# Late values as quarter tiles joined to the next scores, loads ordered by their readers, and the first chunks' tiles kept in weight buffers

## The chip, the cores and the metric

The kernel runs on one core of a Trainium2 chip. The metric is the device time of the whole program in microseconds (us); a run of the kernel before takes 830.32 us (median of three).

## What is computed

Sliding-window attention with a linear bias over 4 batches, 8 heads, 576 positions and head size 64, then two MLPs over the 2304 tokens, all in fp32:

```python
scores = where(0 <= rel < 128, q @ k.T / sqrt(D) - slope_h * rel, -1e9)   # per batch and head
x = softmax(scores) @ v                       # heads side by side: 2304 x 512
h = x @ w_in                                  # 512 -> 2048
x = (max(h, 0) + alpha * min(h, 0)) @ w_out   # 2048 -> 512
h = max(max(x @ w1, x @ w2), x @ w3)          # 512 -> 768
out = h @ w_out2                              # 768 -> 512
```

## The kernel before

The tokens are cut into 9 chunks of 256, joined into five groups of one or two chunks. Attention works on pairs: one chunk and two neighbouring heads, so 36 pairs. For each pair TensorE does three pieces of work. The **scores** (L398) are 8 matmuls of 64 rows by 64 columns, each on one quarter of the array, with 192 moving columns. Then VectorE adds the bias and takes the row minimum (L412), ScalarE exponentiates (L418) and guards the sum (L423), VectorE inverts it (L426), and GpSimd scales the probabilities (L430). The **transposes** (L439) turn the probabilities over by 6 matmuls on the full array; ScalarE copies them to `pt` (L447). The **values** are 8 matmuls with all 128 rows and half of the columns (L459), then 8 on quarters (L466). ScalarE and VectorE split the result into a high and a low part in `x_a` (L479, L481), which the first MLP reads.

Every fp32 weight is likewise split into two parts (ScalarE L344, L346, L362; VectorE L348 to L354; GpSimd L357, L364), and a product of the MLPs is three matmuls (L515 to L517 for the hidden layer, L543 for its output). Jobs run over the hidden blocks f; an item of a job is one f for one or two chunks, that is 256 or 512 moving columns. The attention of chunk 0 stands ahead of the first item, chunk 1 lies within the first job, chunks 2 and 3 within the jobs up to the long one on group 1, and chunks 4 to 8 (`MERGED`) within the later jobs of the first MLP.

All buffers are rings or slots with a planner (`Plan`) that lists every operation with an engine, a cost and a due time, runs a list schedule in both directions for eight rounds, keeps the order with the earliest modelled end, and issues each engine's instructions in that order. Each engine then takes its instructions strictly in order. A buffer's first writer waits for the users of the buffer's last tenant, and, in a ring, also for the first writer of the tile made just before it. The rings that matter here: `qkv` holds the raw queries and keys of two pairs, `v` three, `pt` one, `sb` two PSUM banks. `attend` decides the order in which a pair's pieces are listed: the scores of the new pair, then the transposes and the values of the pair before it. The split weights have 32 buffers of their own, `w`. While the core waits at the start, `keep_busy` (L296) puts 24 matmuls of no use into TensorE's order. A new weight's load waits for the conversion of the fourth weight before it (`AHEAD`).

Of the kernel before, what the change touches and what calls it, by code (L numbers as in the profile page):

```python
# [8 lines left out]
F32 = mybir.dt.float32  # L9
# [61 lines left out]


class Op:
    def __init__(self, eng, cost, due, fn, deps, at, port):
        self.eng, self.cost, self.due, self.fn, self.deps, self.at = eng, cost, due, fn, deps, at
        self.port = port or eng == "pool"


class Plan:

# [8 lines left out]
        self.ops, self.free = [], free  # L89

    def add(self, eng, cost, due, fn, r=(), w=(), after=(), port=False):
        deps = set(after)
        assert not any(b.over for b in (*r, *w))
        for b in r:
            deps.update(b.writers)
        for b in w:
            if not b.writers:
                if b.last:
                    b.last.over = True
                    b.gate.update(b.last.writers, b.last.readers)  # L100
                if b.before and b.before not in w:
                    b.gate.add(b.before.writers[0])
            deps.update(b.gate)
            if b in r:
                deps.update(b.readers)
        op = Op(eng, cost, due, fn, deps, len(self.ops), port)
# [11 lines left out]

    def run(self, due, back=False):

        before, after = {op: list(op.deps) for op in self.ops}, {op: [] for op in self.ops}
        for op in self.ops:
            for d in op.deps:
                after[d].append(op)
        if back:
            before, after = after, before
# [2 lines left out]
        ready, start, end, dma, port = {e: [] for e in free}, {}, {}, 0.0, 0.0  # L129

        def release(op):
            t = max((end[d] + (self.lag(op, d) if back else self.lag(d, op)) for d in before[op]), default=0.0)
            ready[op.eng].append((t, op))

        for op in self.ops:
# [66 lines left out]

APART = (1,)

AHEAD = 4
LATER = 2

# [1 line left out]

KEEP = 3  # L210
ROUNDS = 8
WAIT = 0.08


# [10 lines left out]
def attention_then_two_mlps(ctx: ExitStack, tc: tile.TileContext, qkv, v, w_in, w_out, alpha, w123, w_out2, out):  # L225
# [15 lines left out]
    def either(name, *tiles):  # L241

        pool = ctx.enter_context(tc.tile_pool(name=name, bufs=1))
        return lambda form: pool.tile(*tiles[form], tag=name, name=f"{name}{'abc'[form]}")


    w_s = Slots([either(f"w{i}_", ([P, 2, 512], F32R), ([P, 1024], I32)) for i in range(2 * NF)])
# [4 lines left out]
    o_r = ring("o", 2, ([P, 512], F32))  # L252
    qkv_r = ring("qkv", 2, ([P, 10 * D], F32))
    v_r = ring("v", 3, ([P, 3, 2, D], F32))
    p_r = ring("p", 4, ([P, 2 * R], F32))
    z_r = ring("z", 2, ([P, 16], F32))
    pt_r = ring("pt", 1, ([P, 2, 2 * R], F32))
# [112 lines left out]
    def pair(k, j, hp, due):  # L370


        c = GROUPS[k][j]
        raw, vv, pt, z = qkv_r.new(), v_r.new(), pt_r.new(), z_r.new()
        qs, heads = slice(N + P, 2 * N + P), range(2)
        for a in heads:
            rows = slice(a * D, (a + 1) * D)
            load = add("sp", 0.6, due - 16, lambda a=a, rows=rows: nc.sync.dma_start(
                out=raw()[rows], in_=qkv[2 * hp + a, c, rows, :10 * D]), w=[raw])
# [9 lines left out]
        ps = [p_r.new() for _ in heads]  # L389


        def scores():
# [9 lines left out]
        scored = yield dict(cost=0.8, due=due - 12, fn=scores, r=[raw], w=s)  # L402
        if c == 0:
            idle_b.writers.append(scored)
            keep_busy(2 * KEEP, due - 2, [scored])


        exps = []
        for a in heads:
            for n in range(2):  # L410
                i, p, part = 2 * a + n, ps[a], slice(n * R, (n + 1) * R)
                least = add("dve", 0.28, due - 11 + a, lambda a=a, n=n, i=i, p=p, part=part: nc.vector.tensor_tensor_reduce(  # L412
                    out=p()[:, part], in0=s[a]()[:, part], in1=rel_of(4 * c + n),
                    op0=ALU.add, op1=ALU.min, scale=slope_of(2 * hp + a), scalar=3.0e38, accum_out=z()[:, i:i + 1]),
                    r=[s[a]], w=[p, z])
                if c == 0:
                    idle_b.readers.append(least)
                exps.append(add("act", 0.45, due - 10 + a, lambda i=i, p=p, part=part: nc.scalar.activation(  # L418
                    out=p()[:, part], in_=p()[:, part], func=AF.Exp, scale=-1.0, bias=z()[:, i:i + 1],
                    accum_out=z()[:, 4 + i:5 + i]), r=[p], w=[p, z], after=[least]))  # L420
        for a in heads:
            at_a, two = due - 8 + a, slice(2 * a, 2 * a + 2)
# [3 lines left out]
            share = add("dve", 0.08, at_a, lambda a=a: nc.vector.reciprocal(  # L426
                out=z()[:, 12 + 2 * a:14 + 2 * a], in_=z()[:, 8 + 2 * a:10 + 2 * a]), w=[z], after=[guard])
            for n in range(2):
                i, p, part = 2 * a + n, ps[a], slice(n * R, (n + 1) * R)
                z.readers.append(add("pool", 0.36, at_a + 0.2, lambda i=i, p=p, part=part: nc.gpsimd.tensor_scalar(  # L430
                    out=p()[:, part], in0=p()[:, part], scalar1=z()[:, 12 + i:13 + i], scalar2=1.0,
                    op0=ALU.mult, op1=ALU.mult), r=[p], w=[p], after=[share]))
        yield
        psts = [s_b.new() for _ in heads]
# [5 lines left out]

        if c not in MERGED:
            for a in heads:
                add("pe", 0.36, due - 6.5 + a, lambda a=a: transposes(a), r=[ps[a]], w=[psts[a]])
        else:
            add("pe", 0.7, due - 6, lambda: [transposes(a) for a in heads], r=ps, w=psts)
        for a in heads:
            add("act", 0.38, due - 5.5 + a, lambda a=a: nc.scalar.copy(pt()[:, a, :], psts[a]()[:, :2 * R]),  # L447
                r=[psts[a]], w=[pt])

        psv, at_q = (psts, 2 * R) if c not in APART else ([h_b.new() for _ in range(2)], 0)  # L450


        def values():

            for u in range(2):
                for n in range(2):
                    for a in heads:

                        nc.tensor.matmul(psv[n]()[a * D:(a + 1) * D, at_q + u * D:at_q + (u + 1) * D],  # L459
                                         vv()[:, u + n, a, :], pt()[:, a, n * 2 * P + u * D:n * 2 * P + (u + 1) * D],  # L460
                                         start=(u == 0), stop=False, skip_group_check=True)
            for u in range(2):
                for n in range(2):
                    for a in heads:
                        rows = slice(n * D, (n + 1) * D)
                        nc.tensor.matmul(psv[n]()[a * D:(a + 1) * D, at_q + u * D:at_q + (u + 1) * D],  # L466
                                         vv()[rows, u + 1 - n, a, :], pt()[rows, a, P + u * D:P + (u + 1) * D],
                                         start=False, stop=True, skip_group_check=True)

        yield dict(cost=0.95, due=due - 3.5, fn=values, r=[pt, vv, *(psv if at_q else [])], w=psv)  # L470
# [173 lines left out]
    def put(x):  # L644
        return add("pe", x["cost"], x["due"], x["fn"], r=x["r"], w=x["w"])

    def attend(i):

        for args in sorted(before.get(i, ()), key=lambda args: args is not None):
            new = args and pair(*args)  # L650
            if new:
                scores = next(new)
                new.send(put(scores))
            for one in going:
                put(next(one))
                next(one, None)
            going[:] = [new] if new else []

# [69 lines left out]
```

## Time and profile before

| what | value |
|---|---|
| median of 3 runs (lowest to highest) | 830.32 us (830.13 to 832.75) |
| time of the profiled execution | 833.15 us |
| its span, first to last instruction | 831.4 us |
| TensorE busy in it | 812.2 us |
| ScalarE, VectorE, GpSimd busy | 317.0, 445.6, 202.0 us |
| mean granted TensorE clock | 0.990 of full |

Two engines' busy times can't be added: they work side by side. TensorE is busy for nearly the whole span, so the table asks two questions of every part of the program: is TensorE waiting there, and if not, how long do its own instructions take? In the rows of a timeline, the first number is the start, the second the time from the first start to the last end, and xN counts records; an fp32 matmul of the program leaves two records. Records on one engine overlap, so the pace is read from starts, not from durations.

### The profile page before, as it was taken

The page shows a single profiled execution, that of the slowest core. Times are in us where ns is not written, and L with a number is a line of the kernel's source. Part 1 is how long each engine was busy: PE and PEld are TensorE (multiplying, and loading weights), DVE is VectorE, ACT ScalarE, POOL GpSimd, SP SyncE. Part 2 cuts the span into 40 slices and gives each one's busy share as a digit, 9 for nine tenths or more (in the row PEclk, how much of TensorE's full clock was granted, in tenths as well). Part 3 has the DMA queues.
Part 4 walks back from the last instruction along what each step waited for, and adds up shares of the span by engine and source line. Part 5 has one row for each costly group of instructions (what it writes and reads, how often), then busy time and mean ns, then how long its engine had stood idle before and what let it go on. Part 6 is the DMA issues. An engine that isn't in the chain of part 4 may idle for free.

```text
span 831.4 us, 14008 instructions
## 1 busy us (share of the span) xinstructions
PE 812.2 (98%) x5388; PEld 668.6 (80%) x5388; DVE 445.6 (54%) x1031; ACT 317.0 (38%) x858; POOL 202.0 (24%) x276
## 2 busy tenths in 40 slices
PE   7789999999999999999999999999999999999998
PEld 3678778888778999877787888888888888888897
DVE  4768989963544554544445699994232132222132
ACT  6989874410443443334333565442121121011111
POOL 5767674430121222122100234551000000000000
PEclk9789999999999999999999999999999999999999
DMA  8968530000211321111113774020020020010010
GB/s 241 307 229 264 179 99 14 1 1 0 92 43 52 103 71 53 54 40 43 36 36 122 248 215 140 1 89 13 1 103 1 0 89 13 0 64 13 1 52 26
DMA packets 28724, 65.42 MB, mean 79 GB/s; under 512 B 3824, under 2 KB 9456, under 8 KB 28656
## 3 DMA queue, kind: packets, MB, share of 16 engines
q1 hardware_dynamic: 28656, 64.51, 24.7%
q8 instruction: 43, 0.70, 0.4%
q14 instruction: 25, 0.20, 0.1%
HBM read 54.01 MB, written 10.49 MB: 78 GB/s over the span
## 4 chain that ended last, share of the span: by engine, by line
PE 92%; ACT 3%; DVE 3%; issue 1%; POOL 1%; DMA 0%; SPq 0%; POOLq 0%; DVEq 0%; ACTq 0%
PE xb L543 24%; PE xb L616 9%; PE hb L515 8%; PE hb L516 8%; PE hb L517 8%; PE hb L589 4%; PE sb L589 4%; PE hb L591 4%; PE sb L591 4%; PE sb L590 4%; PE hb L590 4%; PE sb L398 3%; PE sb L439 2%; PE sb L459 2%; PE sb L466 1%; ACT p L418 1%
## 5 line engine op out<-in xcount | busy, mean ns | idle before, releaser
L543 PE MATMUL xb<-g,w_a 128*128 128x512 f32 (+1 forms) x1008 | 221.4, 366 | 1.1 <-ACT g L494 1.1
L543 PEld LDWEIGHTS xb<-g,w_a 128*128 128x128 f32 x1008 | 168.5, 189 | 34.6 <-issue 5.6
L494 ACT CAST g<-hb 128x512 fp32r<-128x512 f32 (+1 forms) x99 | 52.3, 529 | 204.7 <-DVE hb L524 113.1
L515 PE MATMUL hb<-x_a,w_a 128*128 128x512 f32 (+1 forms) x336 | 124.7, 371 | 0.4 <-DVE g L495 0.3
L430 POOL TENSOR_SCALAR p<-p,z 128x192 f32<-128x192 f32 x144 | 66.0, 473 | 232.0 <-DVE z L426 219.0
L516 PE MATMUL hb<-x_a,w_a 128*128 128x512 f32 (+1 forms) x336 | 121.9, 363 | 0.0
L517 PE MATMUL hb<-x_a,w_a 128*128 128x512 f32 (+1 forms) x336 | 121.7, 362 | 0.0
L357 POOL TENSOR_TENSOR wt<-wt,w_b 128x512 int32<-128x512 int32 x56 | 79.5, 1422 | 116.1 <-DVE wt L354 101.1
L521 DVE TENSOR_SCALAR t<-hb,alpha_sb 128x512 f32<-128x512 f32 (+1 forms) x84 | 56.4, 671 | 80.1 <-PE hb L517 80.0
L495 DVE TENSOR_TENSOR g<-hb,g 128x512 fp32r<-128x512 f32 (+1 forms) x99 | 60.9, 616 | 36.7 <-ACT g L494 36.4
L418 ACT ACTIVATE p<-p,z 128x192 f32<-128x192 f32 x144 | 64.2, 447 | 38.6 <-DVE z L412 38.5
L616 PE MATMUL xb<-w_a,g 128*128 128x512 f32 x324 | 78.7, 390 | 0.0
L515 PEld LDWEIGHTS hb<-x_a,w_a 128*128 128x128 f32 x336 | 64.4, 192 | 14.2 <-issue 3.0
L517 PEld LDWEIGHTS hb<-x_a,w_a 128*128 128x128 f32 x336 | 64.5, 192 | 9.6
L516 PEld LDWEIGHTS hb<-x_a,w_a 128*128 128x128 f32 x336 | 64.6, 192 | 8.9
L616 PEld LDWEIGHTS xb<-w_a,g 128*128 128x128 f32 x324 | 60.5, 188 | 12.2
L590 PE MATMUL hb<-x_a,w_a 128*128 128x512 f32 (+1 forms) x180 | 66.3, 368 | 0.0
L591 PE MATMUL hb<-x_a,w_a 128*128 128x512 f32 (+1 forms) x180 | 66.3, 368 | 0.0
L590 PE MATMUL sb<-x_a,w_a 128*128 128x512 f32 (+1 forms) x180 | 66.3, 368 | 0.0
L591 PE MATMUL sb<-x_a,w_a 128*128 128x512 f32 (+1 forms) x180 | 66.3, 368 | 0.0
L589 PE MATMUL sb<-x_a,w_a 128*128 128x512 f32 (+1 forms) x180 | 66.2, 368 | 0.0
L589 PE MATMUL hb<-x_a,w_a 128*128 128x512 f32 (+1 forms) x180 | 66.2, 368 | 0.0
(71 smaller groups left out, 1074.2 us busy)
## 6 DMA issues: line engine op xcount, KB each, us to landing
qkv<-in_qkv SPq DMA_DIRECT2D x72, 160.0 KB, 3.0
w_b<-in_w_out SPq DMA_DIRECT2D x22, 512.0 KB, 5.9
w_b<-in_w SPq DMA_DIRECT2D x18, 512.0 KB, 4.2
w_b<-in_w_in SPq DMA_DIRECT2D x16, 512.0 KB, 6.2
v<-in_v SPq DMA_DIRECT2D x36, 192.0 KB, 2.4
x2d<-o SPq DMA_DIRECT2D x20, 256.0 KB, 2.6
out<-o SPq DMA_DIRECT2D x18, 256.0 KB, 2.1
o<-x2d SPq DMA_DIRECT2D x16, 256.0 KB, 2.9
```

Of the source, the lines that this page charges most:

```text
L357: add("pool", 1.27, due - 5, lambda: nc.gpsimd.tensor_tensor(out=wt().bitcast(I32), in0=wt().bitcast(I32), in1=words(0), op=ALU.add), r=[r ...
L418: exps.append(add("act", 0.45, due - 10 + a, lambda i=i, p=p, part=part: nc.scalar.activation(out=p()[:, part], in_=p()[:, part], func=AF. ...
L430: z.readers.append(add("pool", 0.36, at_a + 0.2, lambda i=i, p=p, part=part: nc.gpsimd.tensor_scalar(out=p()[:, part], in0=p()[:, part], s ...
L495: lo = add("dve", 0.07 + n / 960, due + 0.3, lambda: nc.vector.tensor_tensor(out=g()[:, 1, :n], in0=ps()[:, :n], in1=g()[:, 0, :n].bitcast ...
L515: nc.tensor.matmul(to, wi()[:, 0, ws], x[:, 0, cols], start=(kk == 0), stop=False)
L516: nc.tensor.matmul(to, wi()[:, 1, ws], x[:, 0, cols], start=False, stop=False)
L517: nc.tensor.matmul(to, wi()[:, 0, ws], x[:, 1, cols], start=False, stop=(kk == KD - 1))
L543: nc.tensor.matmul(to, wo()[:, a, ms], g()[:, b, :n], start=(opens and not a and not b), stop=(closes and ends), skip_group_check=apart)
L589: nc.tensor.matmul(to, w()[:, 0, ws], xk[:, 0, :n], start=(kk == 0), stop=False)
L590: nc.tensor.matmul(to, w()[:, 1, ws], xk[:, 0, :n], start=False, stop=False)
L591: nc.tensor.matmul(to, w()[:, 0, ws], xk[:, 1, :n], start=False, stop=(kk == KD - 1))
L616: nc.tensor.matmul(ps, g()[:, a, ts], w()[:, c], start=(opens and not a and not c), stop=(closes and ends))
```

## The change

There are five parts.

1. In the chunks of `MERGED` the values become 24 matmuls on quarters. The 128 keys that were contracted at once are cut into two halves of 64, so each quarter's rows go with one 64-query half. For that the probabilities are written in another order of columns (`part_of_p`), and a second tile `ve` brings the values of the middle part in the other halves of the partitions (two more loads a pair).
2. In those chunks `attend` takes the old pair's transposes first, and then lists the old pair's values and the new pair's scores as one TensorE operation into the same two PSUM banks. Where no pair follows, the values stand alone; where none came before, the scores do.
3. The raw queries and keys and the transposed probabilities of chunks 0 to 3 (`EARLY`) live in the eight last weight buffers, four for each, and not in the rings `qkv` and `pt`.
4. The neighbour in a ring no longer has to end first: it only has to start first (`behind`).
5. A load's due time comes from its earliest reader, 3 us ahead (`DMA_LEAD`). Some modelled costs change, and the order in which a job's last pair is closed.

```diff
@@ Plan.add, Plan.run, Plan.issue
-                if b.before and b.before not in w:
-                    b.gate.add(b.before.writers[0])
+                    behind.add(b.before.writers[0])
...
+                t = max((end[d] + self.lag(d, op) if d in op.deps else start[d] for d in before[op]), default=0.0)
...
+            users = {}
+            for op in self.ops:
+                for d in op.deps:
+                    if d.eng == "sp":
+                        users[d] = min(users.get(d, due[op]), due[op])
+            due.update((d, t - DMA_LEAD) for d, t in users.items())
@@ pair
-        raw, vv, pt, z = qkv_r.new(), v_r.new(), pt_r.new(), z_r.new()
+        vv, z = v_r.new(), z_r.new()
+        if c < EARLY:
+            raw, pt = (w_s.new(2 * NF - 8 + 4 * i + (c * KD + hp) % 4, 2 + i) for i in range(2))
+            ps = [p_r.new() for _ in range(2)]
+        else:
+            raw, pt, ps = qkv_r.new(), pt_r.new(), [p_r.new() for _ in range(2)]
...
+        ve = ve_r.new() if c in MERGED else None
+        if ve:
+            for n in range(2):
+                add("sp", 0.3, due - 9, lambda n=n: nc.sync.dma_start(
+                    out=ve()[n * D:(n + 1) * D], in_=v[hp, c, (1 - n) * D:(2 - n) * D, n * P:(n + 2) * P].rearrange(
+                        "p (k a d) -> p k a d", k=2, a=2)), w=[ve])
...
+        def part_of_p(p, n):
+            if not ve:
+                return p()[:, n * R:(n + 1) * R]
+            return p().rearrange("p (j n r) -> p n j r", n=2, j=3)[:, n]
...
+            def values(psv):
+
+                for u in range(2):
+                    for m in range(3):
+                        for n in range(2):
+                            for a in heads:
+                                rows, of = slice(n * D, (n + 1) * D), ve()[:, u] if m == 1 else vv()[:, u + m // 2]
+
+                                nc.tensor.matmul(psv[n]()[a * D:(a + 1) * D, 2 * R + u * D:2 * R + (u + 1) * D],
+                                                 of[rows, a, :], pt()[rows, a, m * P + u * D:m * P + (u + 1) * D],
+                                                 start=(u == m == 0), stop=(m == 2), skip_group_check=True)
@@ attend
-        for args in sorted(before.get(i, ()), key=lambda args: args is not None):
+        for args in before.get(i, ()):
             new = args and pair(*args)
-            if new:
-                scores = next(new)
-                new.send(put(scores))
+            late = new and going and GROUPS[args[0]][args[1]] in MERGED
+            if new and not late:
+                new.send(put(next(new)))
             for one in going:
-                put(next(one))
+                x = next(one)
+                scores = next(new) if late else None
+                if "w" not in x:
+                    banks, values = scores["w"] if late else [s_b.new() for _ in range(2)], x["fn"]
+                    x.update(fn=lambda: values(banks), w=banks)
+                if late:
+                    first = x["fn"]
+                    new.send(put(dict(cost=1.6, due=x["due"], fn=lambda: (first(), scores["fn"]()),
+                                      r=x["r"] + scores["r"], w=x["w"])))
+                else:
+                    put(x)
                 next(one, None)
```

How the order moves is seen at three places. The first is TensorE's queue in the job on group 2 (chunk 4's successor, one chunk of 256 columns an item). `sb` are the two PSUM banks, `pt` the transposed probabilities, `v` and `ve` the values, `hb` the next hidden block. Before, a pair's values stand by themselves:

```order
L459 MATMUL sb_3692<-pt_3714,v_3351 64x64 x2
L459 MATMUL sb_3696<-pt_3714,v_3351 64x64 x2
L459 MATMUL sb_3692<-pt_3714,v_3351 64x64 x2
L459 MATMUL sb_3696<-pt_3714,v_3351 64x64 x2
L466 MATMUL sb_3692<-pt_3714,v_3351 64x64 x2
L466 MATMUL sb_3696<-pt_3714,v_3351 64x64 x2
L466 MATMUL sb_3692<-pt_3714,v_3351 64x64 x2
L466 MATMUL sb_3696<-pt_3714,v_3351 64x64 x2
L515 MATMUL hb_3742<-x_a,w_a 128x256
```

After, the last six rows of a pair's values (L496) run straight into the next pair's scores (L426) in the same banks:

```order
L496 MATMUL sb_3903<-pt_3900,v_3586 64x64 x2
L496 MATMUL sb_3906<-pt_3900,v_3586 64x64 x2
L496 MATMUL sb_3903<-pt_3900,ve_3707 64x64 x2
L496 MATMUL sb_3906<-pt_3900,ve_3707 64x64 x2
L496 MATMUL sb_3903<-pt_3900,v_3586 64x64 x2
L496 MATMUL sb_3906<-pt_3900,v_3586 64x64 x2
L426 MATMUL sb_3903<-qkv_3685 64x192
L426 MATMUL sb_3906<-qkv_3685 64x192
```

The pass through the MLP's matmuls that stood between values and scores is gone, in 17 of the 20 pairs of `MERGED`; three values and three scores still stand alone.

The second place is ScalarE's queue in the same job. `p` are probabilities, `z` their sums, `g` a hidden block's high part. Before, a pair's exponentials (`p_3654`, `p_3661`) are followed by the copies of the pair before it, whose transposes (of `p_3532`) are in `sb_3692` and `sb_3696`:

```order
L418 ACTIVATE p_3654,z_3655<-p_3654,z_3655 128x192 x2
L418 ACTIVATE p_3661,z_3655<-p_3661,z_3655 128x192 x2
L423 ACTIVATE z_3655<-z_3655 128x2 x2
L447 COPY pt_3714<-sb_3692 128x384
L447 COPY pt_3714<-sb_3696 128x384
L494 CAST g_3719<-hb_3672 128x256
L479 CAST x_a<-sb_3692 128x2x64
L479 CAST x_a<-sb_3696 128x2x64
```

After, they are followed by the copies of the same pair: TensorE transposes `p_3813` into `sb_3877` and `p_3819` into `sb_3881`.

```order
L455 ACTIVATE p_3813,z_3814<-p_3813,z_3814 128x3x64 x2
L455 ACTIVATE p_3819,z_3814<-p_3819,z_3814 128x3x64
L460 ACTIVATE z_3814<-z_3814 128x2
L455 ACTIVATE p_3819,z_3814<-p_3819,z_3814 128x3x64
L460 ACTIVATE z_3814<-z_3814 128x2
L548 CAST g_3875<-hb_3830 128x256
L484 COPY pt_3900<-sb_3877 128x384
L484 COPY pt_3900<-sb_3881 128x384
L548 CAST g_3940<-hb_3887 128x256
```

So a pair's own softmax now lies between its scores and the next TensorE piece of attention, with 36 matmuls of 256 columns of the MLP between them in this job (32 the first time), where before a whole pair lay between. The first guard also moves ahead of the fourth exponential.

The third place is the start of SP's queue of loads. `qkv` or `w_c` are raw queries and keys (two loads a pair), `v` values, `w_b` a raw weight. Before:

```order
L378 DMA qkv_266<-in_qkv 64x640 x2
L382 DMA v_269<-in_v 128x384
L291 DMA alpha_sb<-in_alpha 128x16
L378 DMA qkv_273<-in_qkv 64x640 x2
L342 DMA w_b<-in_w_in 128x1024
L382 DMA v_297<-in_v 128x384
L378 DMA qkv_314<-in_qkv 64x640 x2
L342 DMA w_b<-in_w_out 128x1024
```

After:

```order
L400 DMA w_c<-in_qkv 64x640 x6
L404 DMA v_278<-in_v 128x384
L400 DMA w_c<-in_qkv 64x640 x2
L404 DMA v_297<-in_v 128x384
L404 DMA v_306<-in_v 128x384
L359 DMA w_b<-in_w_in 128x1024
L359 DMA w_b<-in_w_out 128x1024
L400 DMA w_c<-in_qkv 64x640 x2
```

All of chunk 0 now goes ahead of the first weight. Some rows further on, two pairs of chunk 4 (`qkv` and `ve`, loaded into rings that nothing else uses by then) stand before the fifth weight. The eight last weights now wait for the pairs whose tiles hold their buffers; the last load of a weight stands between the stores of the half-finished sum `x2d` at the end of the third job.

## Rows read from the trace of the kernel before

**Rows 1.** The page: span, and busy time of the engines.

```profile
span 831.4 us, 14008 instructions
PE 812.2 (98%) x5388; PEld 668.6 (80%) x5388; DVE 445.6 (54%) x1031; ACT 317.0 (38%) x858; POOL 202.0 (24%) x276
```

**Rows 2.** Busy time by stretch: length, five engines, TensorE's clock, DMA share, GB/s.

```profile
10.00:60.00 50.00, 42.21 (x503) 31.82 (x503) 35.98 (x132) 44.27 (x144) 34.74 (x50) 0.83 0.91 283
...
200.00:440.00 240.00, 240.00 (x2064) 197.36 (x2063) 115.17 (x369) 90.43 (x327) 40.91 (x98) 1.00 0.19 55
```

**Rows 3.** The same columns: both stretches at half clock, and the crowded stretch of loads.

```profile
26.40:36.60 10.20, 9.10 (x70) 7.36 (x71) 6.65 (x25) 8.28 (x26) 9.31 (x14) 0.50 1.04 331
53.70:60.50 6.80, 6.25 (x45) 4.63 (x45) 2.67 (x13) 4.23 (x17) 3.87 (x5) 0.50 0.51 178
...
5.00:55.00 50.00, 42.02 (x493) 29.87 (x497) 35.17 (x131) 44.09 (x145) 33.87 (x53) 0.88 0.96 297
```

**Rows 4.** TensorE's timeline around one pair's scores, and around its values.

```profile
218.12 0.39 PE L517 MATMUL hb<-x_a,w_a 128*128 128x512 f32 x1
218.44 0.88 PE L398 MATMUL sb<-qkv 64*64 64x192 f32 x16
219.25 0.50 PE L515 MATMUL hb<-x_a,w_a 128*128 128x512 f32 x1
219.58 0.40 PE L516 MATMUL hb<-x_a,w_a 128*128 128x512 f32 x1
219.82 0.39 PE L517 MATMUL hb<-x_a,w_a 128*128 128x512 f32 x1
...
224.71 0.69 PE L459 MATMUL sb<-pt,v 128*64 128x64 f32 x16
225.32 0.46 PE L466 MATMUL sb<-pt,v 64*64 64x64 f32 x16
225.71 0.96 PE L543 MATMUL xb<-g,w_a 128*128 128x512 f32 x3
```

**Rows 5.** Records of the attention's lines between 200 and 440 us (ns).

```profile
L398 PE MATMUL sb<-qkv x320: 322/323/374, 208.3 to 422.8; 64*64 64x192 f32 x160
...
L459 PE MATMUL sb<-pt,v x320: 221/222/271, 224.7 to 437.3; 128*64 128x64 f32 x160
...
L466 PE MATMUL sb<-pt,v x320: 217/218/268, 225.3 to 437.6; 64*64 64x64 f32 x160
```

**Rows 6.** Timelines of one softmax with 256 columns an item, and of another.

```profile
292.92 0.88 PE L398 MATMUL sb<-qkv 64*64 64x192 f32 x16
293.73 1.70 PE L543 MATMUL xb<-g,w_a 128*128 128x256 f32 x12
295.27 0.28 PE L515 MATMUL hb<-x_a,w_a 128*128 128x256 f32 x1
295.69 0.44 ACT L418 ACTIVATE p<-p,z 128x192 f32<-128x192 f32 x1
296.13 0.33 ACT L423 ACTIVATE z<-z 128x2 f32<-128x2 f32 x2
296.59 0.28 PE L517 MATMUL hb<-x_a,w_a 128*128 128x256 f32 x1
296.69 1.63 POOL L430 TENSOR_SCALAR p<-p,z 128x192 f32<-128x192 f32 x4 [5.10 <-DVE z L426]
...
286.10 0.74 PE L543 MATMUL xb<-g,w_a 128*128 128x256 f32 x4
...
289.51 1.62 POOL L430 TENSOR_SCALAR p<-p,z 128x192 f32<-128x192 f32 x4 [8.99 <-DVE z L426]
```

**Rows 7.** Timelines early on: ScalarE's fourth hidden block; SP's first weight and first store.

```profile
60.02 0.37 ACT L494 CAST g<-hb 128x256 fp32r<-128x256 f32 x1 [1.23 <-DVE hb L524]
...
4.24 0.58 SPq L342 DMA_DIRECT2D w_b<-in_w_in  x1
...
118.61 1.31 SPq L555 DMA_DIRECT2D x2d<-o  x2
```

More of the change, by code (lines that the diff above doesn't have):

```diff
@@ L91, in add @@
     def add(self, eng, cost, due, fn, r=(), w=(), after=(), port=False):
-        deps = set(after)
+        deps, behind = set(after), set()
         assert not any(b.over for b in (*r, *w))
@@ L105, in add @@
                 deps.update(b.readers)
-        op = Op(eng, cost, due, fn, deps, len(self.ops), port)
+        op = Op(eng, cost, due, fn, deps, behind, len(self.ops), port)
         for b in r:
@@ L119, in run @@
     def run(self, due, back=False):
-        before, after = {op: list(op.deps) for op in self.ops}, {op: [] for op in self.ops}
+        before, after = {op: [*op.deps, *op.behind] for op in self.ops}, {op: [] for op in self.ops}
         for op in self.ops:
-            for d in op.deps:
+            for d in (*op.deps, *op.behind):
                 after[d].append(op)
@@ L131, in release @@
         def release(op):
-            t = max((end[d] + (self.lag(op, d) if back else self.lag(d, op)) for d in before[op]), default=0.0)
+            if back:
+                t = max((end[u] + self.lag(op, u) if op in u.deps else end[u] - op.cost for u in before[op]), default=0.0)
+            else:
+                t = max((end[d] + self.lag(d, op) if d in op.deps else start[d] for d in before[op]), default=0.0)
             ready[op.eng].append((t, op))
@@ L203 @@
 APART = (1,)
+EARLY = 4
 AHEAD = 4
@@ L243, in either @@
         pool = ctx.enter_context(tc.tile_pool(name=name, bufs=1))
[L244 to L247 removed]
+        return lambda form: pool.tile(*tiles[form], tag=name, name=f"{name}{'abcd'[form]}")
+    w_s = Slots([either(f"w{i}_", ([P, 2, 512], F32R), ([P, 1024], I32), ([P, 1024], F32),
+                        ([P, 2, 512], F32)) for i in range(2 * NF)])
     x_s = [Slots([either(f"x{i}{kk}_", ([P, 2, 512], F32R)) for kk in range(KD)]) for i in range(2)]
@@ L410, in pair @@
             for n in range(2):
-                i, p, part = 2 * a + n, ps[a], slice(n * R, (n + 1) * R)
-                least = add("dve", 0.28, due - 11 + a, lambda a=a, n=n, i=i, p=p, part=part: nc.vector.tensor_tensor_reduce(
-                    out=p()[:, part], in0=s[a]()[:, part], in1=rel_of(4 * c + n),
+                i, p = 2 * a + n, ps[a]
+                least = add("dve", 0.28, due - 11 + a, lambda a=a, n=n, i=i, p=p: nc.vector.tensor_tensor_reduce(
+                    out=part_of_p(p, n), in0=like_p(s[a]()[:, n * R:(n + 1) * R]), in1=like_p(rel_of(4 * c + n)),
                     op0=ALU.add, op1=ALU.min, scale=slope_of(2 * hp + a), scalar=3.0e38, accum_out=z()[:, i:i + 1]),
@@ L417, in pair @@
                     idle_b.readers.append(least)
-                exps.append(add("act", 0.45, due - 10 + a, lambda i=i, p=p, part=part: nc.scalar.activation(
-                    out=p()[:, part], in_=p()[:, part], func=AF.Exp, scale=-1.0, bias=z()[:, i:i + 1],
+                exps.append(add("act", 0.45, due - 10 + a, lambda i=i, n=n, p=p: nc.scalar.activation(
+                    out=part_of_p(p, n), in_=part_of_p(p, n), func=AF.Exp, scale=-1.0, bias=z()[:, i:i + 1],
                     accum_out=z()[:, 4 + i:5 + i]), r=[p], w=[p, z], after=[least]))
@@ L448, in pair @@
                 r=[psts[a]], w=[pt])
[L450 to L468, printed above, removed]
@@ L470, in pair, with values @@
-        yield dict(cost=0.95, due=due - 3.5, fn=values, r=[pt, vv, *(psv if at_q else [])], w=psv)
+        if ve:
+            def values(psv):
[7 more added lines that the diff above has]
+                                                 start=(u == m == 0), stop=(m == 2), skip_group_check=True)
+            at_q, handed = 2 * R, dict(cost=0.95, due=due - 3.5, fn=values, r=[pt, vv, ve])
+            yield handed
+            psv = handed["w"]
+        else:
+            psv, at_q = (psts, 2 * R) if c not in APART else ([h_b.new() for _ in range(2)], 0)
+            def values():
+                for u in range(2):
+                    for n in range(2):
+                        for a in heads:
+                            nc.tensor.matmul(psv[n]()[a * D:(a + 1) * D, at_q + u * D:at_q + (u + 1) * D],
+                                             vv()[:, u + n, a, :], pt()[:, a, n * 2 * P + u * D:n * 2 * P + (u + 1) * D],
+                                             start=(u == 0), stop=False, skip_group_check=True)
+                for u in range(2):
+                    for n in range(2):
+                        for a in heads:
+                            rows = slice(n * D, (n + 1) * D)
+                            nc.tensor.matmul(psv[n]()[a * D:(a + 1) * D, at_q + u * D:at_q + (u + 1) * D],
+                                             vv()[rows, u + 1 - n, a, :], pt()[rows, a, P + u * D:P + (u + 1) * D],
+                                             start=False, stop=True, skip_group_check=True)
+            yield dict(cost=1.1, due=due - 3.5, fn=values, r=[pt, vv, *(psv if at_q else [])], w=psv)
```

25 lines of the change are left out of this document (15 added, 10 removed).

## The prediction

> **What bounds the kernel now.** I read the page first: TensorE is busy for 812.2 of 831.4 us [rows 1], so the kernel gets shorter only where TensorE waits, runs at half clock, or spends less on its own instructions. The windows by stretch say which of the three holds where. From 200 to 440 us, where the 20 pairs of chunks 4 to 8 lie, it is busy for all 240.0 us at full clock, with ScalarE at 90.4 and the DMA engines at 0.19 [rows 2]. There only its own instructions count. From 10 to 60 us it is busy for 42.2 of 50, its granted clock averages 0.83, ScalarE is busy for 44.3 and the DMA engines for 0.91 [rows 2]. There two stretches, 10.2 and 6.8 us long, ran at 0.50, the lower of the two levels (1.2 of 2.4 GHz) [rows 3]. That stretch is fed by ScalarE, which has only 5.7 us free in it.
>
> Then I read TensorE's own starts around one pair [rows 4], because its records overlap. The reader is to see that a visit of attention costs more than its matmuls.
>
> **The scores' visit.** Between L517 at 218.12 and L516 at 219.58 lie 1.46 us; two ordinary steps of 0.23 would be 0.46 (L516 to L517 is 0.24 further down), so the scores insert 1.00 us [rows 4]. Their 16 records run on four quarters, so in four rounds. From the first start to the last are 0.88 - 0.32 = 0.56 [rows 4, 5], less 0.02 for the starts within a round: 0.54 for three steps.
>
> **The pace on quarters.** For values, the eight rounds on halves take 0.69 - 0.22 - 0.01 = 0.46 from first to last, the four rounds on quarters 0.46 - 0.22 - 0.02 = 0.22 [rows 4, 5]. With a longer first step f and a steady step p, f + 6p = 0.46 and f + 2p = 0.22: p = 0.06, f = 0.10. So entering a visit costs 0.04 in its first step, the scores' steady step is (0.54 - 0.04) / 3 = 0.167, and four rounds are worth 0.67. Of the scores' 1.00 us, 0.33 is the price of going in and coming out.
>
> **Values on quarters.** Today they take 225.71 - 224.71 = 1.00 us, with one more change of shape inside, at 225.32 [rows 4]. After, 24 matmuls are 48 records in 12 rounds: 0.10 + 10 x 0.06 = 0.70, and as today some 0.16 from the last round to the next product: 0.86. Saved: 0.14 a pair. The bound from below is three times the whole quarter block, 3 x 0.39 = 1.17, a loss of 0.17 a pair. I take 0.86, since the 0.39 holds an entry and an exit that come once.
>
> **Joined to the scores.** 17 of the 20 pairs lose one visit, 0.33 each. Sum of the late part: 17 x (0.14 + 0.33) + 3 x 0.14 = 8.4 us; by the lower bound 17 x 0.33 - 20 x 0.17 = 2.2 us. Nothing hides this, since TensorE has no idle there.
>
> **The softmax that is now between.** What the joining costs: a pair's transposes wait for its own softmax, with 36 matmuls of 256 columns between (32 once). Those matmuls step by 0.12 (11 steps from 295.27 to 296.59) [rows 6], so with 0.1 for the entry the windows are 4.4 us six times and 3.9 us once. In the 512-column jobs they are at least 24 x 0.23 = 5.5 us. The chain today: the scores are done when L543 starts at 293.73, and the last scaling ends at 296.69 + 1.63 = 298.32, so 4.6 us; in the other instance 289.51 + 1.62 - 286.10 = 5.0 us [rows 6]. In the new order the first guard comes ahead of the fourth exponential, that is one exponential (296.13 - 295.69 = 0.44) sooner; GpSimd, free until then, starts 0.4 sooner, and the chain is about 4.2, with the hand-over 4.3. Against 4.4 and 3.9 that is one wait of 0.4. Bounds: none, or with 5.0 each time 6 x 0.6 + 1.1 = 4.7 us. Behind the waiting transposes stand the next hidden block and the values on TensorE's queue, so all of it would reach the end. The new column order changes no size (192 elements); if it made each step a tenth longer, the chain would be 4.7 and the waits 2.6 us, inside these bounds. Late part: 8.4 - 0.4 = 8.0.
>
> **Loads and buffers.** The second values tile is two issues of 64 KB a pair, 2.6 MB in 240 us where the DMA engines are busy for 0.19 [rows 2]; hidden, and if not, 2.6 MB at 297 GB/s [rows 3] is 9 us. The last weights' loads now go out by the store at 118.61 [rows 7], but blocks 12 to 15 are used only after twelve items of 24 x 0.23 = 5.5 us each, some 66 us later: nothing. Starting behind a neighbour instead of ending behind it, and due times of loads, add no instruction.
>
> **The start.** The order shows 1.04 MB more ahead of the first weight, whose load was issued at 4.24 [rows 7], and 0.92 MB of chunk 4 ahead of the fifth. At 297 GB/s, with the DMA engines at 0.96 from 5 to 55 us [rows 3], these are 3.5 and 3.1 us. If ScalarE runs dry for the first, the start is 3.5 us later. The other way, early buffers can win at most ScalarE's free 5.7 us [rows 2]. What stands in ScalarE's order up to its fourth hidden block (at 60.02 before [rows 7]) is four exponentials, three guards and two copies more, and three weight steps less: about 1.5 us more work at 0.44 an exponential [rows 6]. But attention is then a pair further. If half of the idle goes (2.9 us), the block comes 1.4 us sooner. I take +1 us, between -3.5 and +5.7: three scores in a row feed ScalarE early, but eight idle matmuls stand among them.
>
> **The sum.** The profiled execution took 833.15 us over a span of 831.4 [rows 1]; 831.4 - 8.0 - 1 gives a span of 822.4. Its time lies 2.8 us above the median of 830.32, so the saving is taken from the median: 830.3 - 9.0 = 821.3, forecast 821.
>
> **Rivals.**
> - *The start wins as well.* ScalarE's 5.7 us come back, and the second half-clock stretch, 6.25 us of busy TensorE [rows 3], may go with them: 830.3 - 8.0 - 5.7 = 816.6, and down to 814. For it: four pairs' tiles at once. Against: ScalarE is nearly full already.
> - *The softmax takes the place of the visits.* Chains of 5.0 us: 4.7 us of waits instead of 0.4, with no gain at the start 830.3 - 3.7 = 826.6. For it: one of two instances took 5.0. Against: in the new order no hidden block stands between the row minima and the reciprocals on VectorE.
> - *The loads come late.* ScalarE dry for 3.5 us at the start: 830.3 - 8.0 + 3.5 = 825.8. For it: the DMA engines at 0.96. Against: before, the weight was there long before its use.
> - *The quarters don't keep their pace* (the other side). Today's run on quarters is only 16 records, at 0.24 / 15 = 16 ns a record; on halves it is 0.47 / 15 = 31 ns [rows 4, 5]. A run of 48 could fall to the halves' pace if weights for four quarters can't be brought in time: 47 x 0.031 + 0.16 = 1.62 instead of 0.86, 20 x 0.76 = 15.2 us, and 836.5. It decides from 9.0 / 20 / 47 = 10 ns above today's 16, so at 26 ns a record. Against: 16 records in a row show no slowing. The Trainium skill (TensorE: Matmul & The Clock Gate, "Wait — 56ns, not 53.3ns?") states that starts never come closer than about 25 ns, however small the matmul; by that, as an estimate, 47 x 0.025 + 0.16 = 1.34 us, 9.6 us lost and 831. The trace disagrees with it for records on different quarters, with its 16 ns.
>
> **How the numbers follow.** The forecast, late part won and the start within 3 us of today's, gets 0.52, with a range of its own from 818 to 825. The start winning gets 0.20, the softmax 0.13, late loads 0.09, the quarters 0.06. To leave out no more than 2 in 10, the range reaches to 815 into the first rival and to 827 past the next two. A measurement here can tell about 0.3% (2.5 us) from no change. Below 827.8 lie the first four cases, unless the softmax and late loads come together (825.8 + 4.3 = 830.1): faster 0.88; the same 0.05; slower 0.07, the quarters and a start worse than its bounds.
>
> **What would show it.** In the profile after: L496 and L426 in one run, 12 rounds 0.06 apart and no change of shape between; values on quarters about 0.7 us from first to last start; the stretch from the first job of chunk 4 to the end of the attention 8 us shorter at a full TensorE; waits for GpSimd's scaling ahead of the transposes of at most 0.5 us, in the 256-column job alone; ScalarE's fourth hidden block near 59 us. The prediction is wrong if quarter records step by 26 ns or more, if the transposes wait 0.6 us or more each time, or if ScalarE stands idle early for want of weights.

## The result and the profile after

| | before | after |
|---|---|---|
| median of 4 runs each (lowest to highest), us | 831.12 (830.13 to 832.75) | 822.45 (821.81 to 823.44) |
| ratio, 95% interval | | 0.9889 [0.9874, 0.9904] |
| profiled execution: time, span, us | 833.15, 831.4 | 822.61, 820.7 |

By the ratio the change is faster by 9.2 us (1.1%), 8.0 to 10.5 by the interval; the two medians lie 8.7 apart. The forecast was 821.0, inside a range of 815 to 827.

The page after, first its span and busy times as in [rows 1], and then the windows that answer to [rows 2] (length, five engines, TensorE's clock, DMA share, GB/s):

```profile
span 820.7 us, 14638 instructions
PE 799.1 (97%) x5706; PEld 663.7 (81%) x5708; DVE 441.3 (54%) x1031; ACT 319.5 (39%) x858; POOL 203.4 (25%) x276
```

```profile
10.00:60.00 50.00, 39.89 (x502) 29.77 (x505) 34.62 (x133) 43.02 (x148) 34.73 (x54) 0.86 0.84 254
...
200.00:432.00 232.00, 231.82 (x2377) 195.94 (x2376) 115.17 (x361) 90.28 (x317) 39.26 (x93) 1.00 0.22 66
```

In the late stretch TensorE is as full as before and at full clock; it is 8 us shorter because its own instructions take less. In the first stretch TensorE is busy for 2.3 us less than in [rows 2], and still idle for a fifth.

TensorE's timeline after, around one joined pair with 256 columns an item (start, time from the first start to the last end, line, operation, records):

```profile
266.97 0.28 PE L571 MATMUL hb<-x_a,w_a 128*128 128x256 f32 x1
267.18 0.34 PE L496 MATMUL sb<-pt,v 64*64 64x64 f32 x8
267.35 0.30 PE L496 MATMUL sb<-pt,ve 64*64 64x64 f32 x8
267.46 0.41 PE L496 MATMUL sb<-pt,v 64*64 64x64 f32 x16
267.70 0.30 PE L496 MATMUL sb<-pt,ve 64*64 64x64 f32 x8
267.81 0.30 PE L496 MATMUL sb<-pt,v 64*64 64x64 f32 x8
267.93 0.83 PE L426 MATMUL sb<-qkv 64*64 64x192 f32 x16
268.69 0.39 PE L569 MATMUL hb<-x_a,w_a 128*128 128x256 f32 x1
```

L496 (values) and L426 (scores) are one run. The values' last group starts at 267.81 and lasts 0.30; a record lasts 0.218 (below), so the last start is at 267.89, and 48 records start in 0.71 us, 15 ns apart. [Rows 4] had two shapes in 1.00 us there.

```profile
L496 PE MATMUL sb<-pt,v x640: 218/218/267, 214.8 to 425.1; 64*64 64x64 f32 x160
```

The chain of one softmax, from the start of the product behind the scores to the transposes:

```profile
277.31 1.70 PE L597 MATMUL xb<-g,w_a 128*128 128x256 f32 x12
...
280.07 1.63 POOL L467 TENSOR_SCALAR p<-p,z 128x192 f32<-128x192 f32 x4 [6.46 <-DVE z L463]
...
281.73 0.49 PE L476 MATMUL sb<-ident,p 128*128 128x128 f32 x3
```

GpSimd ends at 281.70, 4.39 us behind the scores, and the transposes start 0.03 later, where the products between end anyway. TensorE's waits from 200 to 432 us are a single row, which isn't a transpose:

```profile
PE xb L597 <- ACT o L608: 0.2, 1, 0.2
```

That row lies in the one window with 32 matmuls between scores and transposes:

```profile
271.67 0.64 PE L597 MATMUL xb<-g,w_a 128*128 128x256 f32 x4
272.49 0.82 PE L597 MATMUL xb<-g,w_a 128*128 128x256 f32 x4 [0.18 <-ACT o L608]
273.14 0.82 PE L476 MATMUL sb<-ident,p 128*128 128x128 f32 x6
```

The eight products take 273.14 - 271.67 = 1.47 us there, where eight steps of 0.12 would be 0.96. The window is 4.45 us long (the product behind the scores starts at 268.69), not the 3.9 of the prediction, and so no transpose waits for the softmax, whose scaling GpSimd ends at 273.16.

From 10 to 60 us it still waits often; the longest wait is new and is for a load:

```profile
PE sb L513 <- DMA v<-in_v: 2.6, 1, 2.6
PE sb L476 <- DVE z L449: 2.1, 3, 1.0
PE xb L597 <- ACT g L548: 1.4, 1, 1.4
```

### The profile page after: what moved, and what is told of

It is laid out like the page before. It is cut to its first block, busy times and chain, and to the rows that moved or that the text cites. A ratio compares the mean times of both kernels' runs of the same rounds, so it can differ in the third digit from the quotient of the medians.

```text
span 820.7 us, 14638 instructions
## 1 busy us (share of the span) xinstructions
PE 799.1 (97%) x5706; PEld 663.7 (81%) x5708; DVE 441.3 (54%) x1031; ACT 319.5 (39%) x858; POOL 203.4 (25%) x276
## 4 chain that ended last, share of the span: by engine, by line
PE 93%; ACT 2%; DVE 2%; DMA 1%; POOL 0%; issue 0%; SPq 0%; POOLq 0%; ACTq 0%
PE xb L597 25%; PE xb L670 9%; PE hb L569 8%; PE hb L570 8%; PE hb L571 8%; PE sb L643 5%; PE hb L643 5%; PE hb L644 5%; PE sb L644 5%; PE sb L645 4%; PE hb L645 4%; PE sb L426 3%; PE sb L476 2%; PE sb L496 2%; ACT p L455 1%; DMA v<-in_v 1%
## 5 line engine op out<-in xcount | busy, mean ns | idle before, releaser
L597 PEld LDWEIGHTS xb<-g,w_a 128*128 128x128 f32 x1008 | 170.3, 190 | 36.1 <-issue 5.6
```

The lines of the kernel that those rows point to most:

```text
L597: nc.tensor.matmul(to, wo()[:, a, ms], g()[:, b, :n], start=(opens and not a and not b), stop=(closes and ends), skip_group_check=apart)
```

## A ruler for both parts

Two instants cut every kernel of this study in the same way: the first matmul of hidden item 20 (counting from 0, in the steady products between the early attention and the late) and of hidden item 75, behind the last pair. These are the rows of before, then of after:

```profile
160.19 0.39 PE L515 MATMUL hb<-x_a,w_a 128*128 128x512 f32 x1
...
477.48 0.39 PE L515 MATMUL hb<-x_a,w_a 128*128 128x512 f32 x1
```

```profile
159.55 0.39 PE L569 MATMUL hb<-x_a,w_a 128*128 128x512 f32 x1
...
466.75 0.39 PE L569 MATMUL hb<-x_a,w_a 128*128 128x512 f32 x1
```

One thing has to be put right: in every kernel but before, the first scores of chunk 4 (1.0 us, [rows 4]) already lie ahead of item 20. So the late part fell from 317.29 - 1.0 = 316.3 to 307.20, by 9.1 us, and the start from 160.19 + 1.0 to 159.55, by 1.6. The late part repeats; the start does not. The profile of before is of an execution of 833.15 us, 2.0 above the median, and one and the same order of TensorE's work up to item 20 (idle matmuls aside) gives 159.55 after, 158.41 in after again and 157.38 in quarters alone. Differences of item 20 below some 2 us are therefore not told apart. The half-clock column is the time at the lower level in the first 170 us, summed from windows of half a microsecond.

| kernel | median, us | ratio to before, interval | item 20 | 20 to 75 | half clock, us |
|---|---|---|---|---|---|
| before | 830 to 833 | 1 | 160.19 | 317.29 (316.3) | 17.1 |
| after | 822.45 | 0.9889 [0.9874, 0.9904] | 159.55 | 307.20 | 13.7 |
| quarters alone | 827.22 | 0.9942 [0.9927, 0.9956] | 157.38 | 313.63 | 6.8 |
| joined halves | 824.33 | 0.9902 [0.9886, 0.9918] | 157.96 | 310.60 | 10.2 |
| start only | 831.33 | 0.9982 [0.9971, 0.9992] | 159.90 | 316.33 | 13.7 |
| late only | 828.75 | 0.9962 [0.9949, 0.9976] | 164.82 | 307.97 | 13.7 |
| late part, late order | 823.78 | 0.9904 [0.9886, 0.9921] | 159.74 | 307.95 | 10.2 |
| no early buffers | 827.28 | 0.9950 [0.9930, 0.9969] | 162.96 | 307.20 | 13.7 |
| no due times of loads | 827.39 | 0.9946 [0.9931, 0.9961] | 164.07 | 307.19 | 13.7 |
| chunk 4 held | 822.83 | 0.9891 [0.9872, 0.9910] | 159.72 | 307.20 | 13.7 |
| ten idle matmuls more | 820.79 | 0.9874 [0.9856, 0.9891] | 157.97 | 307.19 | 3.4 |
| held, and ten more | 818.42 | 0.9842 [0.9822, 0.9861] | 155.55 | 307.20 | 0 |
| after again | 821.51 | 0.9880 [0.9864, 0.9896] | 158.41 | 307.20 | 6.8 |

Rows of one batch share runs of before: the four from quarters alone to late only; then late part to chunk 4 held; then the last three.

## The experiments

**1. Which term of the late part is worth what.** Quarters alone: the changed kernel, but values and scores stay two visits.

```diff
-            late = new and going and GROUPS[args[0]][args[1]] in MERGED
+            late = False
```

> The changed kernel, but no pair's values are joined to the next scores; values on quarters, early buffers and load order stay. Theory (visits): the late part keeps only 20 x 0.14 us of its gain, so the time is 831.1 - 2.8 - 1 to 1.6 for the start = 827, 0.994 to 0.996 of the kernel before. Rival (the start): the gain was made before 120 us, so nothing is lost and the time stays at 822 to 823. Rival (quarters): the quarters alone made it, 823 to 824.

Joined halves: the joined operation, with the values in before's form (8 matmuls on halves, 8 on quarters).

```diff
-        ve = ve_r.new() if c in MERGED else None
+        ve = None
```

with the old loop of `values` writing to the banks that it is handed.

> The changed kernel, values joined to the next scores, but in the form of before (8 matmuls on halves, then 8 on quarters; no second values tile, old column order). Theory (visits): 17 x 0.33 = 5.6 us of the late gain stay and 20 x 0.14 = 2.8 are lost: 824.5 to 825.5, 0.992. Rival (quarters): nearly all is lost, 829 or more. Rival (the start): 822 to 823.

Start only: both edits at once, which leaves the early buffers, the starts and the due times, with the new costs and closing order.

> The changed kernel with the late pairs as before (no quarters, no joining): early buffers, starting behind a neighbour and load order alone. Theory (visits): 831.1 - 1 to 1.6 = 829.5 to 830, within 0.3 per cent of before. Rival (the start): 822 to 824.

Late only: the early parts undone, the late ones and the new costs kept.

```diff
-EARLY = 4
+EARLY = 0
...
-                    behind.add(b.before.writers[0])
+                    b.gate.add(b.before.writers[0])
...
-            due.update((d, t - DMA_LEAD) for d, t in users.items())
```

> Quarters and joining alone: the early chunks in the rings as before, the neighbour in a ring has to end first, loads due as before (modelled costs as in the changed kernel). Theory (visits): 831.1 - 8 to 9 = 822 to 823, 0.990. Rival (the start): 829 or more.

Start only took 316.33 from item 20 to 75, the same as before by the ruler, so it is the base line. Against it quarters alone saves 2.70 us, 0.135 for each of 20 pairs, and joined halves 5.73, 0.337 for each of 17 joints. The prediction had 0.14 and 0.33. The median of joined halves came out a little below its expected 824.5 to 825.5, and that of start only above its 829.5 to 830, beside a higher before in this batch (832.74); its ratio, 0.9982, fits. Together they saved 9.13 and not 8.43; the 0.7 between is discussed below. Late only saves 8.3 us in the late part, with two waits for GpSimd in it (0.8 us), but its first part got 3.6 us longer than before's (164.82 against 160.19 + 1.0), and its expectation missed; 828.75 lies near the 829 of the rival, but not for the rival's reason. Its timeline shows where:

```profile
113.93 1.07 PE L425 MATMUL sb<-qkv 64*64 64x192 f32 x16 [0.68 <-DVE x_a L534]
115.83 1.07 PE L475 MATMUL sb<-ident,p 128*128 128x128 f32 x6 [0.83 <-DVE z L448]
...
118.08 0.46 PE L519 MATMUL sb<-pt,v 64*64 64x64 f32 x16
119.78 0.85 PE L475 MATMUL sb<-ident,p 128*128 128x128 f32 x6 [1.23 <-DVE x_a L534]
121.49 1.50 PE L512 MATMUL sb<-pt,v 128*64 128x64 f32 x16 [0.87 <-ACT pt L483]
```

The last pairs of chunk 3 stand in a row, scores, transposes, values, transposes, values, with no product between, and they wait for their softmax, its copies and the splits in the open. TensorE's clock falls as well: from 121 to 128 us it is at 0.51.

**2. Is that bunching the late part's doing, or the order's?** Late part, late order: as late only, but also with before's modelled costs and its order of closing pairs.

```diff
-        scored = yield dict(cost=0.9, due=due - 12, fn=scores, r=[raw], w=s)
+        scored = yield dict(cost=0.8, due=due - 12, fn=scores, r=[raw], w=s)
...
-        for args in before.get(i, ()):
+        for args in sorted(before.get(i, ()), key=lambda args: args is not None):
```

and four more costs in the same way.

> The late part of the change alone (values on quarters, joined to the scores), with the planner's costs, the closing order of jobs and the early buffers, starts and due times all as before. Theory A (two parts that add): the late part saves 8.5 to 9 us from the first job with chunk 4 to the end of the attention, the first 160 us stay within 1.5 us of before, and the median is 8 to 9 below before, at 822 to 824 beside a before of 831 to 832.7. Theory B (the planner puts the early steps in another order whenever costs or handed buffers change): the early attention bunches up as it did with the late part alone and the new costs, the start loses 2 to 4 us, and the median is 826 to 828.5. In both, the late stretch alone is as short as in the changed kernel within 1 us.

Its first theory held in the median: 0.9904, that is 8.0 us (6.6 to 9.5). Items 20 to 75 take 307.95, 8.3 us less and not 8.5 to 9; 0.8 us of that are two waits of one pair's transposes for GpSimd, which the changed order doesn't have:

```profile
PE sb L475 <- POOL p L466: 0.8, 2, 0.4
```

Start only is 1.5 us faster than before (0.7 to 2.4). 8.0 and 1.5 are 9.5, beside 9.2 for the whole change: within the intervals the two parts add, when the early attention isn't bunched.

**3. What of the early part matters.** No early buffers (`EARLY = 0` and nothing else), and no due times of loads (the `due.update` line taken out).

> The changed kernel with the first four chunks' queries, keys and transposed probabilities back in their rotating buffers; everything else as changed. Theory A (the early buffers are what keeps the early attention from bunching and their earlier loads are worth something): the last pairs of chunk 3 stand on TensorE as transposes and values without products between, some 1 to 2 us of waits appear at 100 to 130 us, and the median is 1 to 3 us above the changed kernel, at 823.5 to 825.5. Theory B (the early buffers are worth nothing, or lose because of the 2 MB that they bring ahead): 821 to 823. The late part as in the changed kernel in both.

> The changed kernel without the due times that loads get from their readers. On TensorE the order of the early steps, to the end of chunk 3, is the same as in the changed kernel; loads go out in another order on SyncE. Theory A (the order of the loads decides the early waits): the wait of 2.6 us for the fourth pair's values, or others like it, change, and the median moves by 1 to 3 us, up or down, against 822.5. Theory B (TensorE's order and ScalarE decide): within 1 us of 822.5. Both: the late part as in the changed kernel.

Both lose more than was expected: the medians, of another batch, lie 4.8 and 4.9 us above the changed kernel's, with the late part unchanged to 0.01 us. Without the early buffers two pairs stand bunched at 115 to 125 us, with one wait of 1.5 us, and TensorE's clock is 0.66 in the next 5 us. Without due times it isn't only the loads that go out in another order, as its expectation had it: ScalarE's order differs from 14 us on and TensorE's from 36 us on. These are TensorE's rows after, then without due times:

```profile
36.36 1.08 PE L476 MATMUL sb<-ident,p 128*128 128x128 f32 x6 [0.84 <-DVE z L449]
37.61 0.54 PE L426 MATMUL sb<-w_c 64*64 64x192 f32 x2 [0.18 <-ACT w_d L484]
```

```profile
35.87 0.52 PE L475 MATMUL sb<-ident,p 128*128 128x128 f32 x3 [1.02 <-DVE z L448]
37.77 1.90 PE L596 MATMUL xb<-g,w_a 128*128 128x256 f32 x8 [1.38 <-ACT g L547]
```

From 35 to 75 us it then waits for ScalarE's hidden blocks four times, where the changed kernel does once, for 1.4 us (above):

```profile
PE xb L596 <- ACT g L547: 3.9, 4, 1.4
```

So taking one of these two away costs 4.8 us together with the new order that the planner finds without it, and neither run prices its part by itself. All early parts together give 1.5 us (start only), and the late part with the late order, which has none of them, reaches item 20 at 159.74, within 0.2 us of the changed kernel.

**4. The wait for the load.** Chunk 4 held: the loads of chunk 4 and later, and all second values tiles, go out only after chunk 3's first scores.

```diff
-                out=raw()[rows, :10 * D], in_=qkv[2 * hp + a, c, rows, :10 * D]), w=[raw])
+                out=raw()[rows, :10 * D], in_=qkv[2 * hp + a, c, rows, :10 * D]), w=[raw], after=hold if c >= EARLY else ())
...
+        if c == EARLY - 1 and not hold:
+            hold.append(scored)
```

> The changed kernel with one dependence more: the loads of chunk 4 and later, and all second values tiles, go out only after chunk 3's first scores, so that they don't stand ahead of the first chunks' loads. In the changed kernel TensorE waits 2.61 us, at 27 us, for the values of the fourth pair, whose load was issued at 19.83 and landed 7.0 us later, behind chunk 4's. Theory A (the early loads collide, and this wait reaches the end): that wait is gone and the median is 1.5 to 2.6 us below the changed kernel's 822.5, at 820 to 821. Theory B (how soon ScalarE gets its work sets the first 60 us, and the waits only move): the wait on the values is gone, but another one takes its place, and the median stays within 1 us of 822.5. The late part, from the first job after the early attention to its end, stays as in the changed kernel in both.

The second theory held. Of TensorE's wait for values 0.6 us is left of 2.6, but item 20 is at 159.72, not sooner, and the half clock is as long as in the changed kernel. TensorE's order differs here too, from 39 us on.

**5. The clock.** In the changed kernel TensorE is busy for 1.2 of the 4 us from 22 to 26, its clock falls there, and it is at 0.50 for most of the next 10 us and again near 40:

```profile
22.00:26.00 4.00, 1.17 (x22) 0.82 (x20) 1.06 (x4) 3.31 (x9) 4.00 (x5) 0.92 0.87 208
26.00:36.00 10.00, 7.85 (x76) 6.05 (x76) 5.38 (x19) 5.32 (x18) 6.39 (x9) 0.52 0.70 252
38.50:42.50 4.00, 4.00 (x28) 3.38 (x28) 2.47 (x12) 3.11 (x11) 3.44 (x6) 0.57 1.00 278
```

Ten idle matmuls more, behind the transposes of the fourth pair:

```diff
-                add("pe", 0.3, due - 6.5 + a, lambda a=a: transposes(a), r=[ps[a]], w=[psts[a]])
+                turned = add("pe", 0.3, due - 6.5 + a, lambda a=a: transposes(a), r=[ps[a]], w=[psts[a]])
+            if c == 0 and hp == KD - 1:
+                keep_busy(10, due - 5, [turned])
```

> The changed kernel with ten idle matmuls more after the transposes of the first chunk's fourth pair; the order has five of them ahead of that pair's values, where TensorE waited 2.61 us for a load, and five behind them. In the changed kernel the granted clock falls to 0.50 at 24 to 26 us, behind a patch where TensorE was busy for 1.2 of 4 us, and stays there for some 10 us. Theory A (the idle patch costs the clock, and the clock costs time): the clock falls later or for a shorter stretch, item 1 of the hidden blocks starts 1 to 3 us sooner, and the median is 820 to 821.5. Theory B (ScalarE sets the first 60 us, half clock or not): the clock is better and the median is within 1 us of the changed kernel's 822.5. If the planner, which now has ten costs more, places the early attention worse, 823.5 or more.

The numbers are those of its first theory: 3.4 us at half clock, item 1 at 42.80 us instead of 45.71, and 820.79 us. But the changed kernel itself, once more in the same batch (below), has item 1 at 44.57 and 821.51 us, 0.7 away with overlapping intervals, and TensorE's order with the ten matmuls differs from 13 us on. The theory is not shown by it.

Held, and ten more:

> Both edits at once: the loads of chunk 4 and the second values tiles held back until chunk 3's first scores, and ten idle matmuls more after the transposes of the fourth pair. Holding alone gave 822.83. Theory A (load wait and clock were two halves of one loss): 819 to 821. Theory B (ScalarE sets the first 60 us): within 1 us of 822.5.

After again, the changed kernel itself:

> The changed kernel itself once more, for a second profile beside the two above. Theory A (the start varies between executions of one program by which stretches run at half clock): the profile shows another pattern of half clock in the first 50 us than the 13.7 us of the first profile, and item 20 of the hidden blocks starts more than 0.5 us away from 159.55. Theory B (the pattern belongs to the program): the same stretches within 1 us, item 20 within 0.5 us. The late part, item 20 to 75, takes 307.2 us within 0.1 in both. Median 822 to 823.

Its first theory held: 6.8 us at half clock instead of 13.7, and item 20 at 158.41. The median, 821.51, lies 0.5 below what was expected.

With both edits the timeline and the same windows are:

```profile
23.64 0.84 PE L478 MATMUL sb<-ident,p 128*128 128x128 f32 x6 [1.22 <-DVE x_a L539]
24.32 1.25 PE L313 MATMUL xb<-ident 128*128 128x512 bf16 x5
26.56 1.06 PE L517 MATMUL sb<-w_d,v 128*64 128x64 f32 x16 [0.99 <-ACT w_d L488]
27.55 0.46 PE L524 MATMUL sb<-w_d,v 64*64 64x64 f32 x16
27.94 1.26 PE L313 MATMUL xb<-ident 128*128 128x512 bf16 x5
```

```profile
22.00:26.00 4.00, 2.35 (x28) 1.38 (x27) 3.47 (x7) 2.93 (x7) 4.00 (x5) 1.00 0.95 275
26.00:36.00 10.00, 7.35 (x93) 4.84 (x93) 9.12 (x29) 9.14 (x31) 7.52 (x9) 1.00 0.93 307
38.50:42.50 4.00, 3.67 (x39) 3.03 (x38) 3.54 (x9) 3.97 (x15) 3.10 (x6) 1.00 0.41 122
```

No stretch at half clock is left in the first 170 us of this profile, ScalarE is busy for 9.1 of the 10 us from 26 to 36 instead of 5.3, item 20 comes 2.9 us before that of after again, and the median is 818.42 beside 821.51 in the same batch. That is the fastest kernel of the study, 1.6% below before, and its interval ends below that of after again. The first theory was right there, beyond its own bound of 819. Each edit alone is not told apart from the changed kernel (820.79 and 822.83, intervals that overlap with it). The planner also orders the early steps a little differently in each of these kernels, so how much of the 3.1 us is the clock alone is not shown.

## Why the prediction was right

**The quarters' pace** held. 16 ns a record was read from runs of 16; runs of 48 gave 15. The rival that needed 26 ns is out. The Trainium skill (TensorE: Matmul & The Clock Gate, "Wait — 56ns, not 53.3ns?") states that starts never come closer than about 25 ns; for fp32 records on different quarters these 15 ns decide against it.

**The visits** were priced rightly one by one (0.135 and 0.337 measured, 0.14 and 0.33 predicted), but the sum was under-sized: 8.4 predicted (8.0 after a wait of 0.4 that didn't come), 9.1 measured. The missing 0.7 us shows only with both at once. Joined halves and after have the same items in the same order from item 20 to 75, and no wait that differs. Summed from the starts of TensorE's records, it lies in the ordinary steps of the 512-column products: the same 923 of them take 213.53 us in joined halves and 213.11 after, while the same 912 take 212.29 in start only and 212.63 in quarters alone. Why those steps differ stays open.

**The softmax between** took its place without a wait. To GpSimd's end the chain measured 4.39 us where 4.2 was predicted (4.3 with the hand-over), still inside the cover of 4.4, with 0.03 to spare: that it fits is in part luck. The single wait of 0.4, in the window with 32 matmuls, didn't occur because TensorE lost about that time in the same window already, waiting for ScalarE's `o` (above). In the late part with the late order two such waits of 0.4 are there.

**The start** was put at +1 between bounds. The profiles give 1.6 and 2.8 (after, after again), both against the one profile of before, 2.0 us above its median. What the late part's 9.1 leaves of the measured gain is 0.1 (of 9.2), or 0.9 by after again (of 10.0); start only, in another early order, gives 1.5. So +1 is inside what was measured, and no run tells it better. That the forecast's 9.0 stands so close to 9.2 owes something to luck: the late part gave 1.1 more than its 8.0, and by this remainder the start gave 0.9 less. The reason given for the start was only half right. The sign that was to show it failed: ScalarE's fourth hidden block starts at 63.3, the last of the four in the row below, not near 59, and so 3.3 us later than in [rows 7]; the attention is ahead by then, as predicted by a pair: 40 exponentials begun in the first 60 us instead of 36. ScalarE's hidden blocks after, from 25 to 75 us (durations, first and last start):

```profile
L548 ACT CAST g<-hb x4: 350/354/372, 39.0 to 63.3; 128x256 fp32r<-128x256 f32 x4
```

ScalarE was never dry for want of weights for 3.5 us, as the rival of late loads had it; from 5 to 75 us its longest wait for a weight's load is 0.7. A load was late all the same, the fourth pair's values at 27 us, for 2.61 us; the prediction named no load of values.

**What it didn't see** is how much hangs on the order: the same late part with another early order (late only) gives 828.75, and no term of the sum stood for that.

## What to carry to other kernels

Price a visit to another tile shape from a timeline, as time inserted between two ordinary steps, apart from the records' own pace; here removing 17 such visits was worth twice what a better shape for 20 was. In a stretch that several engines share, a wait taken away may only move: here holding loads back, or filling the idle patch, was not told from nothing, and both together, with another order besides, gave 3.1 us. When a planner sets the order, test a part of a change also with the old order held, or its price is mixed with that of a reshuffle; and compare the orders of all engines, since taking out the loads' due times moved them all here.

## What the runs showed of the hardware

The same program has different stretches at half clock from one execution to the next: 13.7 us in the first profile of the changed kernel and 6.8 in the second. Item 20 moved by only 1.14 us between them. The price isn't the same everywhere: of the 38 executions of before that ran beside the experiments, the 24 with a mean granted clock of 0.990 or 0.991 have spans of 830.1 to 831.7 us, and the 14 with 0.993 to 0.995 have 828.3 to 829.5. In the kernel with both edits of experiment 5, the two executions at 0.997 have 817.4 and 817.7, the three at 0.999 have 815.4 to 816.7. Whether the clock makes these differences, or a late start that also lowers the clock, is not shown.

The late part, at full clock, repeated within 0.01 us in seven profiles (after, after again and five variants of the early part).
